# One queue for batch 0's x, a hold on GpSimd's loads, the first layer in halves, and a new order: cross-attention followed by a snake layer on one core

## The chip, the cores and the metric

The kernel runs on one NeuronCore of a Trainium2 chip. The core has TensorE (PE in the profile: matmuls and transposes into eight PSUM banks), ScalarE (ACT), VectorE (DVE), GpSimd (POOL) and SyncE (SP). Transfers are started from queues: SP and ACT start plain copies ("hardware" queues in the profile), GpSimd starts copies that also change the type from fp32 to bf16 (the "software" queue). All of them run on the same 16 DMA engines.

The metric is the time of one execution on the device in microseconds. The kernel before takes 228.31 us, the median of 3 runs (228.03 to 229.27).

## The reference

```python
x:     (8, 8, 512, 64)    # batch, head, token, dim
state: (8, 8, 32, 64)
scores = x @ state^T / sqrt(64);   a  = softmax(scores);   xread = a @ state
scores2 = state @ x^T / sqrt(64);  a2 = softmax(scores2);  sread = a2 @ x
X = concat([xread, sread], tokens) -> (8*544, 512)     # heads side by side

h = X @ w_in                    # 512 -> 2048
g = h + sin(alpha*h)**2 / (alpha + 1e-9)
out = g @ w_out                 # 2048 -> 512
```

Both softmaxes come from the same exponentials E, normalized along states for `xread` and along tokens for `sread`.

## The kernel before

**Tiling.** There are nine token tiles `t`. Tile 0 to 7 is `xread` of batch `t` (512 tokens), tile 8 holds the 256 rows of `sread` of all batches. The 2048 hidden units are 16 blocks `f` of 128. For each pair (t, f) the kernel makes `h` (two matmuls of 128x512 for a batch, four of 128x256 for tile 8), then `si` (sine on ACT), `sq` (square on ACT "A", DVE "V" or GpSimd "G"), `gt` (square times 1/alpha plus h, on DVE, which frees the PSUM bank of h). The output is made in row blocks `o.t.st`, each a chain of 16 matmuls over f into one bank, copied out by `oc` and stored by `os` on SP.

**M instead of xread.** For a batch, a @ state @ w_in is computed as A^T times M, with M = state @ w_in per pair of heads. `m.b.s` makes slice s (512 of the 2048 columns) of M in two PSUM banks, one for each half g of the contraction (four heads each), and `me` copies each to bf16. `h` then sums over g = 0 and g = 1. The A of a batch has the same two halves.

**Batch 0's start.** x of batch 0 comes in quarters (`lq`, two heads each, fp32, 256 KB), is cast and rearranged (`xq`), transposed on TensorE (`xtq`), copied to SBUF (`xc`), multiplied with the transposed state (`sc`), then `ex` (exponential on ACT), `rs` and `rr` (sum and reciprocal on DVE), `nm` (normalize on DVE or GpSimd), `at` (transpose on TensorE), `ac` (copy). State 0 comes by its own small load (`l_st0`), is transposed by `st0_t` and copied into the state tile `stT` by `st0_c`. The states of the other batches come in one load `l_st`, transposed by `st_t` and copied by `st_c`.

**The other batches.** `lx` loads x on GpSimd's queue as bf16, `pk` rearranges it on DVE, `td` transposes it by DMA on SP (batch 1 does it on TensorE, `xt`), and `ad` transposes A by DMA on SP. `w`, `cs`, `rc` and `xs` make `sread` of a batch.

**Weights.** `li.s` loads slice s of w_in (columns, 512 KB as bf16), `lo.s` loads four blocks f of w_out, all on GpSimd's queue in the order of the list.

**Order.** Each engine executes its instructions in the order in which they were emitted, and waits when an input is not there or a buffer is not free. The emission order is a written list of steps, `ORDER`, in which a step's arguments name batch, block, PSUM bank and engine. For example `h.0.7.4` is h of tile 0, block 7, in bank 4; `o.0.1.3.4` adds block 3 to row block 1 of tile 0; `m.1.3.6.3` is slice 3 of batch 1 into banks 6 and 3. There is no other scheduler. `warm_up.n.cols.bank` issues n matmuls of zeros that nothing reads. The start of the list:

```python
lq.0.A lq.1.S consts lq.2.A l_st0 zero.0 ident_ warm_up.6.512.0 zero.1 exp_table lq.3.S l_st
identf.V li.0 l_alpha xq.0.V li.1 xtq.0.1 xq.1.A li.3 xq.2.A xtq.1 xc.0.0.0.V st0_t.2 lx.1.0.1
xc.0.0.1.A xtq.2.3 st0_c.0.A warm_up.2.128.4 xq.3.V st0_c.1.A warm_up.2.128.5 lo.0 xc.0.1.0.V xtq.3
```

Lines that the profile names: L234 `lq`, L228 `l_st0`, L240 `l_st`, L248 `lx`, L255 `li`, L261 `lo`, L270 `warm_up`, L298 `st_t`, L313 `pk`, L321 `xq`, L328 `xtq`, L353 `xc`, L359 `td`, L369 `sc`, L376 `ex`, L401 `at`, L407 `ac`, L411 `ad`, L459 `m`, L467 `me`, L484 `h` of a batch, L490 `h` of tile 8, L498 `si`, L507 `sq` on ACT, L195 products on GpSimd or DVE (`sq`, `nm`), L514 `gt`, L525 `o`, L533 `oc`, L540 `os`.

Of the kernel before, what the change touches and what calls it, by code (L numbers as in the profile page):

```python
# [13 lines left out]
FP32 = mybir.dt.float32  # L14
# [19 lines left out]
sq.0.15.A xc.1.1.1.V o.0.1.0.1.7 sq.0.14.G gt.0.4 o.0.1.1.2 sc.1.1.3 si.0.12 o.0.1.2.3 gt.0.15
o.0.1.3.4 o.0.0.0.1.1 ex.1.0 sq.0.12.G o.0.0.1.2 gt.0.14 o.0.0.2.4 o.0.1.4.6 pk.1.0.V o.0.1.6.7
gt.0.12 o.0.1.7.8 h.0.13.6 ex.1.1 rs.1.0 o.0.0.4.5 o.0.2.3.4 si.0.13 o.0.2.4.5 rr.1.0 o.0.2.5.6
rs.1.1 o.0.2.6.7 nm.1.0.0.4.G m.0.2.0.4 m.1.2.2.3 rr.1.1 o.0.0.5.6 me.0.2.0.V o.0.0.6.7 nm.1.1.0.4.G
o.0.2.7.8 me.0.2.1.A me.1.2.0.V o.0.0.7.8 o.0.3.0.1.0 sq.0.13.A o.0.3.1.2 me.1.2.1.V h.0.8.4 ad.1
h.0.9.2 gt.0.13 si.0.8 h.0.10.3 si.0.9 o.0.3.2.3 sq.0.8.V o.0.3.3.4 h.0.11.6 si.0.10 gt.0.8 sq.0.9.G
o.0.3.4.6 si.0.11 o.0.3.6.7 o.0.1.8.9 sq.0.10.A h.1.2.4 gt.0.9 sq.0.11.G o.0.0.8.9 o.0.3.7.8 si.1.2  # L40
gt.0.10 h.1.12.2 lx.3.0.1 o.0.3.8.9 gt.0.11 sq.1.2.A h.1.7.3 o.0.0.9.10 si.1.12 gt.1.2 h.1.4.6
si.1.7 o.0.0.10.11 sq.1.12.V o.0.1.9.10 h.1.13.4 pk.2.0.V si.1.4 sq.1.7.G gt.1.12 o.0.1.10.11
o.0.0.11.12 si.1.13 o.0.0.12.14 sq.1.4.A o.0.0.14.15 pk.2.1.V sq.1.13.G h.1.8.2 gt.1.7 td.2
o.0.2.8.10 si.1.8 gt.1.4 o.0.0.15.16 h.1.3.3 oc.0.0.A gt.1.13 sq.1.8.G o.0.3.9.10 h.1.0.6 si.1.3
os.0.0 h.1.14.1 si.1.0 gt.1.8 sq.1.3.G o.0.1.11.13 si.1.14 h.1.1.4 h.1.5.2 sq.1.0.G si.1.1
o.0.3.10.12 si.1.5 o.0.2.10.11 sq.1.14.G o.0.1.13.15 sq.1.1.A o.0.1.15.16 o.0.3.12.14 oc.0.1.A
sq.1.5.G pk.3.1.V pk.3.0.V gt.1.3 td.3 gt.1.0 gt.1.1 h.1.6.3 h.1.9.6 os.0.1 gt.1.14 si.1.6
o.0.3.14.15 sc.2.1.7 gt.1.5 si.1.9 sc.2.0.4 sq.1.6.G o.0.2.11.13 ex.2.0 o.0.2.13.15 sq.1.9.G
o.0.2.15.16 gt.1.6 o.0.3.15.16 o.1.3.0.2.1 oc.0.2.V o.1.3.2.4 h.1.10.2 oc.0.3.A gt.1.9 os.0.2
o.1.1.0.1.3 ex.2.1 o.1.1.1.2 os.0.3 rs.2.0 h.1.11.5 si.1.10 o.1.1.2.3 rr.2.0 m.2.0.4.0.6.7 rs.2.1  # L50
nm.2.0.0.4.G o.1.1.3.4 rr.2.1 o.1.1.4.5 me.2.0.1.V o.1.1.5.6 nm.2.1.0.4.G o.1.3.4.5 me.2.1.1.A
o.1.3.5.6 o.1.1.6.7 si.1.11 o.1.3.6.7 o.1.1.7.8 sq.1.10.G me.2.1.0.V me.2.0.0.V ad.2 o.1.3.7.8
sq.1.11.A o.1.3.8.10 h.1.15.0 gt.1.11 o.1.2.0.2.7 si.1.15 o.1.2.2.3 gt.1.10 o.1.2.3.5 sq.1.15.A
o.1.2.5.6 o.1.1.8.10 gt.1.15 m.2.2.6.4.5.2 o.1.1.10.11 me.2.2.0.A me.2.2.1.V h.2.1.0 me.2.3.0.A
o.1.1.11.12 me.2.3.1.V h.2.3.6 si.2.1 o.1.1.12.14 si.2.3 h.2.13.4 sq.2.1.V h.2.0.5 gt.2.1 sq.2.3.A
w.0.2 si.2.0 gt.2.3 cs.0 h.2.2.0 si.2.13 rc.0 sq.2.0.G o.1.2.6.7 o.1.1.14.15 si.2.2 o.1.2.7.9
sq.2.13.G xs.0.0 h.2.5.6 sq.2.2.A gt.2.0 o.1.1.15.16 o.1.2.9.10 si.2.5 o.1.2.10.11 oc.1.1.V lx.4.0.1
h.2.10.5 sq.2.5.A gt.2.13 o.1.2.11.12 os.1.1 h.2.4.3 si.2.10 xs.0.1 o.1.2.12.13 o.1.0.0.1.4 gt.2.5
si.2.4 sc.3.0.2 sq.2.10.G o.1.0.1.3 gt.2.2 h.2.8.6 sq.2.4.A o.1.2.13.14 gt.2.10 h.2.15.0 si.2.8
o.1.0.3.4 gt.2.4 o.1.2.14.15 si.2.15 sq.2.8.G sc.3.1.5 o.1.0.4.5 o.1.2.15.16 ex.3.0 o.1.0.5.6  # L60
o.1.3.10.11 sq.2.15.G oc.1.2.V o.1.0.6.8 gt.2.8 o.1.0.8.9 os.1.2 o.1.0.9.10 h.2.7.3 gt.2.15
o.1.3.11.12 ex.3.1 o.1.0.10.11 pk.4.1.V o.1.3.12.13 si.2.7 o.1.0.11.12 rs.3.0 o.1.3.13.14
o.1.0.12.14 rs.3.1 m.3.2.7.6.2.0 o.1.3.14.15 pk.4.0.V o.1.3.15.16 rr.3.0 me.3.2.0.A o.1.0.14.15 td.4
rr.3.1 sq.2.7.G me.3.3.0.V h.2.11.5 oc.1.3.A o.1.0.15.16 me.3.2.1.V h.2.9.7 me.3.3.1.A nm.3.0.0.4.G
h.2.6.2 oc.1.0.A gt.2.7 o.2.0.0.1.1 os.1.3 si.2.11 o.2.0.1.2 os.1.0 nm.3.1.0.4.G o.2.0.2.3
m.3.0.0.6.4.3 si.2.9 o.2.0.3.4 si.2.6 sq.2.11.G me.3.0.1.V ad.3 o.2.0.4.6 me.3.1.1.A me.3.0.0.V
o.2.1.0.1.6 me.3.1.0.A o.2.1.1.2 sq.2.9.G o.2.1.2.3 gt.2.11 h.2.14.3 sq.2.6.A o.2.1.3.5 si.2.14
gt.2.9 sc.4.0.0 sc.4.1.4 gt.2.6 o.2.1.5.6 sq.2.14.A h.2.12.5 ex.4.0 o.2.2.0.1.7 gt.2.14 o.2.2.1.3
o.2.0.6.11 o.2.1.6.7 si.2.12 rs.4.0 o.2.0.11.12 o.2.1.7.8 h.3.0.2 rr.4.0 h.3.5.3 nm.4.0.0.4.V
# [532 lines left out]
```

The softmax here doesn't subtract the row's maximum and nothing guards it: scores larger than these inputs give would overflow.

## Time and profile before

| | |
|---|---|
| median of 3 runs | 228.31 us (228.03 to 229.27) |
| profiled execution | 228.42 us |
| its span | 226.7 us |
| busy: TensorE | 212.7 us, 94% |
| busy: ACT, DVE, GpSimd | 176.5, 162.6, 113.1 us |
| granted TensorE clock | 1.00 throughout |
| HBM read, written | 17.38 MB, 8.91 MB |
| DMA, first 26 us | 200 GB/s |
| first o matmul | 26.12 us |
| last matmul chain to end of span | 222.97 to 226.7 us |

Busy time counts the time in which at least one instruction of the engine is under way. A group's mean includes the time from issue to result, so a matmul of 512 columns is listed with some 379 ns although ten in a row take 2.16 us. In a line of the timeline the first number is the start, the second the length of the merged group, then engine, source line, operation, output and input, the count, and in brackets how long the engine had been idle and what ended that. Lines of windows give, for a stretch from A to B, the busy time and count of each engine in the order PE, PEld (weight loads), DVE, ACT, POOL, then granted clock, DMA share and GB/s. A line of a DMA queue gives packets, MB, and its share of 16 engines' time in the window; q0 is GpSimd's queue, q1 SP's and q10 ACT's.

### The profile page before, as it was taken

Reading aid. Unit: us, or ns where it says so; the run is one execution under the profiler, and the core shown is the slowest. Engines: PE = TensorE matmul, PEld = TensorE weight load, DVE = VectorE, ACT = ScalarE, POOL = GpSimd, SP = SyncE. Lnnn points to the kernel's source line nnn. Section 1 sums busy time; section 2 is a strip of 40 time slices with the busy share of each in tenths; the row PEclk is TensorE's granted clock in tenths of the full one; section 3 lists DMA queues with packets and bytes.
Section 4 is the critical chain, followed back from the end, with each engine's and each line's share of the span. In section 5 each row is a group of like instructions: output and inputs, shape, how many; then the busy total and the mean of one; then the engine's idle time right before and its main releaser. Section 6 shows DMA issues by size and latency. Waiting matters only on the chain.

```text
span 226.7 us, 4202 instructions
## 1 busy us (share of the span) xinstructions
PE 212.7 (94%) x1538; PEld 104.6 (46%) x1565; DVE 162.6 (72%) x282; ACT 176.5 (78%) x296; POOL 113.1 (50%) x123
## 2 busy tenths in 40 slices
PE   4599899999999899999999999989999999999993
PEld 1473544444444344444444444444455656557441
DVE  3268997998897958888898888798368558782000
ACT  3299988998899899889997599799573789981122
POOL 8436955885064714844965358546033329461000
PEclk9999999999999999999999999999999999999999
DMA  7999993974136730774348710870104111110222
GB/s 175 213 202 206 206 174 55 174 189 123 19 62 127 171 64 0 196 140 85 35 58 229 145 50 0 130 193 5 46 0 154 36 46 49 46 48 3 94 83 102
DMA packets 37949, 23.42 MB, mean 103 GB/s; under 512 B 21016, under 2 KB 33576, under 8 KB 37928
## 3 DMA queue, kind: packets, MB, share of 16 engines
q0 software_dynamic: 11648, 8.13, 25.1%
q1 hardware_dynamic: 25704, 14.49, 23.6%
q10 hardware_dynamic: 576, 0.53, 0.8%
q8 instruction: 12, 0.20, 0.3%
q14 instruction: 9, 0.07, 0.1%
HBM read 17.38 MB, written 8.91 MB: 116 GB/s over the span
## 4 chain that ended last, share of the span: by engine, by line
PE 65%; DVE 8%; ACT 8%; DMA 7%; POOL 6%; issue 4%; SPq 0%; POOLq 0%; ACTq 0%
PE o_ps L525 41%; PE h_ps L484 13%; POOL s L195 5%; ACT s L498 5%; DMA x<-in_x_dram 4%; DMA xnat<-in_x_dram 4%; DVE gT L514 3%; PE h_ps L490 3%; PE m_ps L459 2%; DVE xp L313 2%; PE s_ps L369 2%; PE w_ps L421 1%; ACT M L467 1%; DVE M L467 1%; PE w_ps L432 1%
## 5 line engine op out<-in xcount | busy, mean ns | idle before, releaser
L525 PE MATMUL o_ps<-w_out_sb,gT 128*128 128x512 bf16 (+1 forms) x540 | 131.6, 373 | 2.1 <-DVE gT L514 0.8
L195 POOL TENSOR_TENSOR s<-s 128x512 bf16<-128x512 bf16 (+1 forms) x88 | 86.2, 997 | 72.2 <-ACT s L498 65.6
L514 DVE SCALAR_TENSOR_TENSOR gT<-s,inva_sb,h_ps 128x512 bf16<-128x512 bf16 (+1 forms) x144 | 97.0, 713 | 21.6 <-POOL s L195 12.8
L498 ACT ACTIVATE s<-h_ps,alpha_sb 128x512 bf16<-128x512 f32 (+1 forms) x144 | 89.1, 671 | 9.9 <-PE h_ps L484 8.5
L525 PEld LDWEIGHTS <-gT 128*128 128x128 bf16 x560 | 53.0, 98 | 61.9 <-issue 4.6
L484 PE MATMUL h_ps<-AT,M 128*128 128x512 bf16 x249 | 70.3, 379 | 2.1 <-DVE M L467 0.7
L484 PEld LDWEIGHTS <-M 128*128 128x128 bf16 x256 | 24.4, 98 | 31.8 <-issue 4.7
L507 ACT ACTIVATE s<-s 128x512 bf16<-128x512 bf16 (+1 forms) x49 | 29.9, 611 | 0.8
L533 ACT COPY o_sb<-o_ps 128x512 f32<-128x512 f32 (+1 forms) x25 | 14.2, 574 | 20.1 <-PE o_ps L525 20.1
L467 ACT CAST M<-m_ps 128x512 bf16<-128x512 f32 x34 | 18.4, 594 | 5.4 <-PE m_ps L459 5.4
L195 POOL TENSOR_TENSOR A<-E,rR 128x512 bf16<-128x512 bf16 x13 | 13.4, 1047 | 17.5 <-DVE rR L386 11.8
L467 DVE CAST M<-m_ps 128x512 bf16<-128x512 f32 x30 | 19.2, 676 | 2.9 <-PE m_ps L459 2.8
L380 DVE TENSOR_REDUCE R<-E 128x16 f32<-128x512 bf16 x16 | 10.5, 664 | 3.4 <-ACT E L376 3.4
L459 PE MATMUL m_ps<-w_in_sb,stT 64*32 64x512 bf16 x256 | 10.8, 382 | 0.1
L376 ACT ACTIVATE E<-s_ps 128x512 bf16<-128x512 f32 x16 | 9.2, 599 | 1.6 <-PE s_ps L369 1.6
L498 ACT ACT_TABLE_LOAD x7 | 9.0, 1283 | 0.9 <-PE h_ps L484 0.8
L376 ACT ACT_TABLE_LOAD x7 | 9.0, 1283 | 0.1
L490 PE MATMUL h_ps<-xs_all,w_in_sb 128*128 128x256 bf16 x64 | 8.6, 272 | 0.0
L313 DVE COPY xp<-xnat 128x1024 bf16<-128x1024 bf16 x14 | 7.8, 575 | 1.1 <-DMA xnat<-in_x_dram 1.1
L533 DVE COPY o_sb<-o_ps 128x512 f32<-128x512 f32 x10 | 6.9, 686 | 2.3 <-PE o_ps L525 2.1
L439 DVE RECIPROCAL rC<-w_ps 128x128 f32<-128x128 f32 x8 | 7.5, 946 | 1.4 <-PE w_ps L432 1.4
L490 PEld LDWEIGHTS <-w_in_sb 128*128 128x128 bf16 x64 | 6.3, 98 | 2.8 <-issue 0.2
(54 smaller groups left out, 90.8 us busy)
## 6 DMA issues: line engine op xcount, KB each, us to landing
out_dram<-o_sb SPq DMA_DIRECT2D x33, 256.0 KB, 2.4
xnat<-in_x_dram POOLq DMA_DIRECT2D x7, 512.0 KB, 6.1
w_in_sb<-in_moe_w_in_dram POOLq DMA_DIRECT2D x4, 512.0 KB, 12.3
w_out_sb<-in_moe_w_out_dram POOLq DMA_DIRECT2D x4, 512.0 KB, 18.0
x<-in_x_dram ACTq DMA_DIRECT2D x2, 256.0 KB
x<-in_x_dram SPq DMA_DIRECT2D x2, 256.0 KB, 5.8
st_nat<-in_state_dram POOLq DMA_DIRECT2D x1, 256.0 KB, 7.2
out_dram<-o_sb SPq DMA_DIRECT2D x2, 128.0 KB
```

What stands on the lines that cost most here:

```text
L195: {"V": k.nc.vector, "G": k.nc.gpsimd}[eng].tensor_tensor(out, a, b, ALU.mult)
L313: k.copy(eng)(k.t["xp", b][:, :, hs, :], k.t["xnat", b][:, hs, :].rearrange("p h (i d) -> p i h d", i=k.C),)
L376: k.nc.scalar.activation(E[:, g], k.t["sc", b, g][:], ACT.Exp, scale=k.scale)
L459: k.nc.tensor.matmul(k.t["m", b, s + n, g][o0:o0 + k.Ns, :], k.stT[k.half(r), b * k.G + g, c0:c0 + k.Ns], k.w_in_sb[k.half(r), 2 * g + h, ...
L467: k.copy(eng)(k.t["M", b][:, g, s * k.FW:(s + 1) * k.FW], k.t["m", b, s, g][:])
L484: k.nc.tensor.matmul(hp[:, :n], k.t["M", t][:, g, fs], k.t["AT", t][:, g, :], start=(g == 0), stop=(g == k.G - 1),)
L490: k.nc.tensor.matmul(hp[:, :n], k.w_in_sb[:, q, fs], k.xs_all[:, q].rearrange("p b j -> p (b j)"), start=(q == 0), stop=(q == k.Q - 1),)
L498: k.nc.scalar.activation(s[:, :n], k.t["h", t, f][:, :n], ACT.Sin, scale=k.alpha_sb[:, f:f + 1])
L507: k.nc.scalar.activation(s2[:, :n], s[:, :n], ACT.Square)
L514: k.nc.vector.scalar_tensor_tensor(gT[:, :n], k.t["s2", t, f][:, :n], k.inva_sb[:, f:f + 1], k.t["h", t, f][:, :n], ALU.mult, ALU.add,)
L525: k.nc.tensor.matmul(k.t["o", t, st, half][:, cols], k.t["gT", t, f][:, rows], k.w_out_sb[:, f, cols], start=(f == 0), stop=(f == k.FT - 1),)
L533: k.copy(eng)(o_sb[:, cols], k.t["o", t, st, half][:, cols])
```

## The change

- The four quarters of batch 0's x are all issued on SP, in order, and the state of batch 0 and now also that of batch 1 are loaded by SP (`l_sf`, transposed by `sf_t`, copied by `sf_c`). `l_st` still brings all states; its copies now serve batches 2 to 7.
- A new step `hold` makes GpSimd copy one column of quarter 0, so GpSimd goes on to its loads only when that quarter has landed. The loads follow in the order w_in 0, 2, 1, x of batch 1, w_out 0, 1, all states, then (behind both `nm` of batch 0) w_in 3, w_out 2, 3, x of batch 2.
- `h` of batch 0 is issued as two steps `hg`, one for each half g of the contraction, which may stand apart in the list.
- There are 18 `warm_up` steps instead of 6: the first with 6 matmuls of 512 columns as before, then 17 with 2 of 128 columns (before 5).
- Both `nm` of batch 0 are on GpSimd (one was on DVE).
- The whole list is new. Batches are worked in the order 0, 1, 2, 3, 5, 4, 7, 6 with tile 8 (before 0 to 7, then 8 beside 7), banks and engines of the copies and squares are chosen anew (squares: 43 on ACT, 78 on GpSimd, 7 on DVE before; 48, 69, 11 after, for tiles 0 to 7; output copies of whole rows: 23 on ACT and 10 on DVE before, 15 and 18 after; M copies: 34 and 30 before, 39 and 25 after). The row block made in two halves (`oh`) is now one of tile 7.

```diff
-lq.0.A lq.1.S consts lq.2.A l_st0 zero.0 ident_ warm_up.6.512.0 zero.1 exp_table lq.3.S l_st
-identf.V li.0 l_alpha xq.0.V li.1 xtq.0.1 xq.1.A li.3 xq.2.A xtq.1 xc.0.0.0.V st0_t.2 lx.1.0.1
...
+l_alpha lq.0.S consts lq.1.S zero.0 ident_ exp_table warm_up.6.512.0 zero.1 l_sf.0.S lq.2.S identf.V
+lq.3.S l_sf.1.S xq.0.A hold li.0 xtq.0.1 xq.1.A li.2 sf_t.0.2 xc.0.0.0.V al_t.3 li.1 xq.2.A xtq.1
+sf_c.0.1.V sf_c.0.0.V al_c xtq.2.4 xc.0.0.1.A xq.3.V lx.1.0.1 inva xtq.3 xc.0.1.0.A sc.0.0.5 lo.0
+xc.0.1.1.V sf_t.1.6 ex.0.0 sc.0.1.7 lo.1 sf_c.1.1.V sf_c.1.0.A warm_up.2.128.0 rs.0.0
+warm_up.2.128.2 ex.0.1 l_st warm_up.2.128.3 warm_up.2.128.1 rr.0.0 warm_up.2.128.4 sin_table rs.0.1
+warm_up.2.128.5 nm.0.0.0.4.G m.0.0.6.0 m.1.0.2.3 rr.0.1 warm_up.2.128.7 me.0.0.1.V warm_up.2.128.1
+warm_up.2.128.4 warm_up.2.128.5 nm.0.1.0.4.G at.0.0.7 me.1.0.1.A me.0.0.0.V warm_up.2.128.1
+warm_up.2.128.4 warm_up.2.128.5 warm_up.2.128.0 ac.0.0.A warm_up.2.128.1 warm_up.2.128.4 me.1.0.0.V
+warm_up.2.128.3 li.3 at.0.1 hg.0.1.0.5 hg.0.2.0.0 ac.0.1.V m.1.2.6.1 lo.2 hg.0.3.0.4 me.1.2.0.A
+me.1.2.1.V hg.0.2.1 lo.3 hg.0.3.1 hg.0.1.1 si.0.2 m.0.2.3.2 lx.2.0.1 hg.0.0.0.7 si.0.3 me.0.2.1.V
+hg.0.0.1 me.0.2.0.A m.0.1.6.1 sq.0.3.V sq.0.2.G si.0.1 gt.0.3 hg.0.10.0.2 hg.0.9.0.3 si.0.0 hg.0.9.1
+me.0.1.0.V sq.0.1.G hg.0.10.1 hg.0.8.0.4 me.0.1.1.A hg.0.8.1 hg.0.5.0.6 si.0.10 hg.0.5.1 sq.0.0.G
+gt.0.2 gt.0.1 hg.0.4.0.1 hg.0.4.1 si.0.5 hg.0.7.0.0 hg.0.7.1 sq.0.10.A xt.1.0.5 pk.1.1.V sq.0.5.G
+gt.0.0 si.0.4 gt.0.10 xt.1.1.7 xc.1.0.1.A sq.0.4.G xc.1.0.0.V si.0.9 hg.0.6.0.2 xc.1.1.0.V hg.0.6.1
+xc.1.1.1.A gt.0.5 o.0.3.0.1.5 sq.0.9.G o.0.3.1.2 si.0.6 o.0.3.2.3 gt.0.4 o.0.3.3.4 o.0.1.0.1.7
...
-        e = k.stT[:, 0:k.G] if part == 0 else k.stT[:, k.G:]
+        e = k.stT[:, 0:2 * k.G] if part == 0 else k.stT[:, 2 * k.G:]
...
-    def l_st0(k):
-        k.st0 = k.const.tile([k.Ns, k.H, k.D], FP32, name="st0")
-        k.nc.sync.dma_start(k.st0[:], k.state[0].rearrange("h j d -> j h d"))
+    def l_sf(k, b, eng):
+        k.t["sf", b] = k.const.tile([k.Ns, k.H, k.D], FP32, name=f"sf{b}")
+        {"A": k.nc.scalar, "S": k.nc.sync}[eng].dma_start(
+            k.t["sf", b][:], k.state[b].rearrange("h j d -> j h d")
+        )
...
+    def hold(k):
+        k.nc.gpsimd.tensor_copy(k.tiny[:, 2:3], k.x0[:, 0, 0:1])
...
-    def st0_t(k, bank):
+    def sf_t(k, b, bank):
...
-    def st0_c(k, r, eng):
+    def sf_c(k, b, r, eng):
...
-        k.copy(eng)(dst[:, k.Q:, r, :, half, :], src[:, k.Q:, r])
+        k.copy(eng)(dst[:, 2 * k.Q:, r, :, half, :], src[:, 2 * k.Q:, r])
...
+    def hg(k, t, f, g, *bank):
+        if g == 0:
+            k.t["h", t, f] = k.ps(bank[0], [k.P, k.S], FP32, "h_ps")
+        k.nc.tensor.matmul(
+            k.t["h", t, f][:], k.t["M", t][:, g, f * k.P:(f + 1) * k.P], k.t["AT", t][:, g, :],
+            start=(g == 0), stop=(g == k.G - 1),
+        )
```

## The prediction

> **What bounds the kernel now.** I read the page first (engine shares, slices), then the timeline of the first 26 us, the DMA queues in half-microsecond windows, the landing times of the weights, and last the count of TensorE weight loads from the start to several times.
>
> ```profile
> PE 212.7 (94%) x1538; PEld 104.6 (46%) x1565; DVE 162.6 (72%) x282; ACT 176.5 (78%) x296; POOL 113.1 (50%) x123
> ...
> PE   4599899999999899999999999989999999999993
> ```
>
> TensorE is the bound, except in the first slices. There the timeline shows what it waits for:
>
> ```profile
> 4.08 0.62 ACT L321 CAST xp<-x 128x512 bf16<-128x512 f32 x1 [0.78 <-DMA x<-in_x_dram]
> 4.64 0.90 DVE L321 CAST xp<-x 128x512 bf16<-128x512 f32 x1 [2.33 <-DMA x<-in_x_dram]
> 5.56 0.62 ACT L321 CAST xp<-x 128x512 bf16<-128x512 f32 x1 [0.86 <-DMA x<-in_x_dram]
> 8.90 0.74 POOL L261 DMA_DIRECT2D w_out_sb<-in_moe_w_out_dram  x1 [1.37 <-DMA st_nat<-in_state_dram]
> 10.10 0.43 DVE L321 CAST xp<-x 128x512 bf16<-128x512 f32 x1 [3.00 <-DMA x<-in_x_dram]
> 12.01 1.19 ACT L376 ACTIVATE E<-s_ps 128x512 bf16<-128x512 f32 x2
> ```
>
> Three quarters of batch 0 are there by 5.6 us, the fourth at 10.1, and the first exponential follows at 12.0. The queues, in the windows 2.5:3.0 and 5.0:5.5, say why:
>
> ```profile
> q1 hardware_dynamic: 96, 0.10, 57.1%
> q10 hardware_dynamic: 78, 0.08, 44.8%
> ```
> ```profile
> q0 software_dynamic: 25, 0.05, 58.4%
> q1 hardware_dynamic: 13, 0.01, 9.6%
> ```
>
> SP's queue moves 96 packets in half a microsecond beside ACT's, and 13 once GpSimd's queue is running.
>
> ```profile
> 0.00:26.00 26.00, 19.25 (x193) 10.90 (x196) 15.24 (x34) 17.84 (x33) 16.20 (x24) 1.00 1.13 200
> ...
> 0.00:75.00 75.00, 66.87 (x519) 32.36 (x528) 59.08 (x108) 63.17 (x103) 44.70 (x52) 1.00 0.81 146
> ...
> 0.00:155.00 155.00, 145.39 (x1086) 68.50 (x1105) 127.06 (x220) 134.25 (x219) 91.11 (x98) 1.00 0.65 125
> ```
>
> The weight loads say how far the order has come. I price TensorE's steps by chain rows: an o matmul 0.216 (10 in 2.16), an h pair 0.43, a slice of M 0.28 (16 matmuls in 0.56), one sc call 0.235, w 0.47, cs 0.57, st_t 0.95, an h of the last tile 0.44. By these, the first 196 loads are worth 14.1 us at 26, 528 are worth 61.0 at 75, and 1105 are worth 139.8 at 155. The kernel is behind its own TensorE work by 11.9, 14.0 and 15.2 us. So nearly all that is lost is lost before the first o matmul at 26.12. From there 193.7 us of work remain and TensorE ends at 222.97, 196.85 later: 3.1 lost. The last copy and its store take 3.73 more, to the span of 226.7.
>
> **The change part by part.** The sum is made against the profiled execution, 228.42 (226.7 and 1.72 around it); the median of the runs, 228.31, is 0.11 below.
>
> *x on SP alone.* SP issues in 0.46 each: quarters 0 and 1 from 0.74, batch 0's state, quarters 2 and 3, batch 1's state (from 3.05). The two added issues and the second state load put 1.4 us in front of nothing else on SP, whose next work before was at 33.48. ACT loses two issues (1.04); its exponential table still ends before quarter 0 is there. 1.18 MB at the 0.13 to 0.18 MB per half microsecond that the hardware queues moved before 4.5 us, from first packets at 2.2: quarter 0 at 3.3, quarter 3 at 5.5 to 6.6. I take 6.3, as one queue alone moved 0.14 in the window 4.0:4.5.
>
> *The hold.* One GpSimd copy of a column waits for quarter 0; queued behind it are all GpSimd loads, so the first issue moves from 1.44 to about 3.5. The first load's packets came 3.1 us after its issue (1.44 to 4.5), so GpSimd's packets start at about 6.7, when quarter 3 is through. The whole st_nat load (256 KB) also goes behind five other loads. The first slice of w_in landed 9.6 us after its issue at 2.17, at 11.8; the next loads fit steps of 2.56 us (512 KB at the 205 GB/s of the windows):
>
> ```profile
> DMA to landing us min/median/max: 9.6/12.3/20.4
> ```
>
> After: w_in slice 0 at 9.8 (6.7, 2.56 and half a microsecond for completion), slice 2 at 12.4, slice 1 at 15.0, batch 1's x at 17.5, w_out's first two parts at 20.1 and 22.7, st_nat 24.0, slice 3 at 26.5, the last w_out at 31.7. Before, by the same steps: 11.8, 14.4, 16.9 for the first three slices, x 19.5, w_out 22.0, 24.6, its last 32.2. So the weights come 0.5 to 2 us earlier although they are asked for later.
>
> A rule that speaks against one queue: the Trainium skill, "DMA: Bandwidth & Descriptors", section "Queues, rings and completion order", says that every DMA engine goes round the queues packet by packet. Once GpSimd runs, two x queues would then hold two turns of three, one queue one of two. By the rule alone the sum goes towards the last rival below, 229.9; by the rows it stays, as quarter 3 is through by 6.7.
>
> *Batch 0's chain.* Quarter 3 at 6.3, cast and transposes to 7.5, scores and first exponential at 8.1 to 8.7 (12.0 before). A second state transpose sits before the second scores (0.5). Sums and reciprocals (0.69 and 0.25 each) bring the first GpSimd normalization to 9.9; the second is now also GpSimd's, 1.05 behind it instead of DVE's 0.67 beside it (to 12.0). M's first slices wait for w_in, 9.8. The second half of AT is copied at 13.2, so the first full h is at 13.4; it was 17.3 to 18.1. The split into halves lets the first half's matmul start 0.6 earlier; it adds no matmul, and I give it nothing, as ACT is the limit next. Twelve more spare matmul steps (24 matmuls, 1.3 us warm) stand before the first h, in time in which TensorE waits anyway; should they be on the path, they cost 1.3, and at the half rate of the first six (0.43 each) 2.6.
>
> A second rule: "TensorE: Matmul & The Clock Gate", Part 1, says the array runs at half rate until some 3.4 us of sustained work. In the trace four transposes take 0.61 at 14.88 and 0.40 at 15.94, which looks like that step, while the granted clock reads 1.00. By the rule, the 22 half matmuls of the first h's would cost up to 4.7 more if the array fell idle before them, and the spare matmuls prevent that; by the rows, where the longest wait is 2.75 (8.16 to 10.91), there is nothing to prevent and no term.
>
> *To the first o.* ACT then runs without a gap: M copies (0.59), sines (0.69), squares (0.64) and x copies (0.62), from 13.3: si.0.2 13.9, si.0.0 to 17.1, sq.0.10 to 19.6, the last x copies 20.8 and 22.1. DVE's gt.0.10 (0.74) after that square ends at 20.6, which frees the bank of hg.0.6; o.0.3 follows at 21.1 to 21.7, and I take 21.4 (26.12 before). Landing bounds it from below: w_out's first part, 20.1. From above: 23.4, if quarter 3 comes at 8.3.
>
> *The rest.* At the first o the new order has less behind it: 195.9 us of work remain, not 193.7 (both state transposes, 1.9, and one more slice of M, 0.28, come later). All o, h, w and cs counts are equal. Other moves: 5 M copies, 8 squares to ACT, 8 output copies from ACT to DVE, 13 squares off GpSimd, one pair of table loads fewer (2.57); ACT's sum changes by under 1 us of 176.5. ACT (78%) must now keep up with a TensorE that is 4 us nearer. I take 3.1 lost as before plus 0.4; ends 2 and 6.
>
> Sum: 21.4 + 195.9 + 3.5 = 220.8; with 3.73, span 224.5; with 1.72, 226.3; on the scale of the median **226.2**, 2.1 less than 228.31.
>
> **The rivals.**
> - *The weights bind.* If the GpSimd stream only shifts by the 2.1 of the hold, less the 1.3 that st_nat's 256 KB takes, w_in lands at 12.6 and w_out at 22.9, and the first o waits: 22.9 + 195.9 + 3.5 + 3.73 + 1.72 = 227.8. For it: the loads did share their first microseconds with x. Against: that sharing cost them throughput too, and it is gone.
> - *ACT takes it back.* ACT is busy 43.8 of the first 54 us and 63.2 of 75. If it can't give more, the lost time grows from 3.5 to 6: 228.7, no change.
> - *Late x loads (slower).* The order issues the x of batches 3 to 7 only 6.0 to 6.9 us of TensorE work before the DVE copy that reads it (before: 6.4 to 8.8). The median landing is 6.1, but the one issued at 63.99 took 8.05, and between 70 and 75 us the lag grew by 0.8. If all five land as late at 0.8 to 1.0 each, 4 to 5 us are added, of which one was in the 3.1: 229.4 to 230.3. It decides from four late loads of five. Against it: only one load of six did so.
> - *Quarter 3 is starved anyway.* If one queue can't finish x before GpSimd starts, quarter 3 comes at 10 and everything moves by 3.7: 229.9.
>
> **How the numbers follow.** Forecast 0.58 (own range 224.5 to 227.7), weights 0.12, ACT 0.11, late x 0.13, starved quarter 0.06. The range 224.2 to 230.0 runs from an early first o (20.1) with 3 lost to the slower rivals. A measurement can tell about 0.5%, 1.14 us: faster is below 227.2, slower above 229.45. Most of the forecast (0.55), a third of the weights and little of ACT are faster: 0.62. Slower: late x, starved x, a little of ACT: 0.21. The rest, 0.17.
>
> **What would show it.** Right: the last cast of x at about 6.5 without a DMA wait of 3 us; the first exponential near 8.5; first h near 13.4; first o near 21.4; a lag, in weight loads priced as above, near 8 at the first o and below 12 at the end; the same 3.7 tail. Wrong: M's first matmuls after 12 (weights), DVE copies of x waiting for DMA in batches 3 to 7, or a lag that grows by more than 5 after 25 us.

## The result and the profile after

The changed kernel takes 237.1 us (median of four runs, 235.2 to 238.2) against 228.2 for the kernel before on the same chip: a ratio of 1.038, 95% interval 1.031 to 1.046. It is 8.9 us slower; the forecast was 2.1 us faster. The profiled execution took 235.16 us, with a span of 233.2. It is the fastest of the four, so the trace shows 6.7 us of the loss; the numbers below are of that execution.

The page, with the lines that answer to those shown of before (TensorE's share, its busy tenths in 40 slices), and the chain that ended last, by engine:

```profile
PE 217.2 (93%) x1593; PEld 105.3 (45%) x1593; DVE 166.1 (71%) x289; ACT 176.8 (76%) x299; POOL 105.1 (45%) x114
...
PE   5889998999989797999999959999999999999993
...
PE 62%; DMA 17%; ACT 9%; POOL 5%; DVE 3%; issue 3%; POOLq 0%; ACTq 0%
```

The same chain of the kernel before:

```profile
PE 65%; DVE 8%; ACT 8%; DMA 7%; POOL 6%; issue 4%; SPq 0%; POOLq 0%; ACTq 0%
```

The first slices are fuller than before (5889 against 4599). But there are now dents in the middle (an 8 and two 7s in slices 12 to 16, a 5 in slice 24), where the kernel before had hardly anything under 9. And DMA holds 17% of the chain that sets the end; before it was 7%.

The timeline of the start of the changed kernel (start, length, engine, line, operation; in brackets the idle time before and what ended it):

```profile
3.78 1.38 ACT L335 CAST xp<-x 128x512 bf16<-128x512 f32 x2 [1.08 <-DMA x<-in_x_dram]
7.42 0.43 DVE L335 CAST xp<-x 128x512 bf16<-128x512 f32 x1 [0.17 <-DMA x<-in_x_dram]
9.03 0.60 ACT L390 ACTIVATE E<-s_ps 128x512 bf16<-128x512 f32 x1
...
3.93 2.42 POOL L267 DMA_DIRECT2D w_in_sb<-in_moe_w_in_dram  x3
...
12.38 1.05 PE L473 MATMUL m_ps<-w_in_sb,stT 64*32 64x512 bf16 x16 [1.06 <-DMA w_in_sb<-in_moe_w_in_dram]
13.37 1.04 PE L282 MATMUL warm_ps<-warm 128*128 128x128 bf16 x8
14.20 0.63 PE L415 MATMUL a_ps<-ident,A 128*128 128x128 bf16 x4
14.62 1.41 PE L282 MATMUL warm_ps<-warm 128*128 128x128 bf16 x14
15.87 0.39 PE L415 MATMUL a_ps<-ident,A 128*128 128x128 bf16 x4
16.10 0.59 PE L513 MATMUL h_ps<-AT,M 128*128 128x512 bf16 x2
```

x does come early: the last cast is at 7.4 instead of 10.1, the first exponential at 9.0 instead of 12.0. Then TensorE waits for the first slice of w_in (12.38), and 22 spare matmuls (1.04 and 1.41 us) stand in its queue ahead of the two transposes of A. The first half layer is at 16.1, the first o matmul at 24.8 (26.1 before): 1.3 us are won.

The windows from the start (busy time and count for PE, PEld, DVE, ACT, POOL; granted clock, DMA share, GB/s) say where it is lost again:

```profile
0.00:26.00 26.00, 21.35 (x189) 11.92 (x190) 16.34 (x36) 16.57 (x29) 17.77 (x26) 1.00 1.05 186
0.00:65.00 65.00, 58.91 (x492) 29.11 (x492) 48.93 (x92) 51.64 (x86) 37.32 (x45) 1.00 0.93 156
0.00:75.00 75.00, 68.82 (x551) 33.38 (x552) 57.21 (x105) 60.80 (x103) 44.72 (x53) 1.00 0.89 153
0.00:95.00 95.00, 86.05 (x660) 40.69 (x661) 73.29 (x131) 76.14 (x129) 52.90 (x61) 1.00 0.82 140
0.00:130.00 130.00, 121.05 (x908) 56.75 (x909) 99.35 (x175) 107.77 (x178) 70.57 (x78) 1.00 0.71 126
0.00:140.00 140.00, 128.02 (x974) 60.28 (x974) 105.96 (x187) 113.78 (x187) 72.74 (x80) 1.00 0.71 126
```

Priced as in the prediction, the weight loads are worth 15.0, 51.9, 62.0, 78.4, 113.2 and 120.1 us. The lag (the time less that work) is 11.0, 13.1, 13.0, 16.6, 16.8 and 19.9 us. From there to the end it is flat: 19.2 at 220 us. In the kernel before it went from 11.9 to 14.8 over the whole run. So the start is better, and some 8.7 us are lost between 34 and 140 us.

The waits of 34 to 145 us that DMA ended (engine, line, what was waited for; total us, times, longest), and the links of DMA in the chain that ended last (issue, us to landing):

```profile
DVE xp L327 <- DMA xnat<-in_x_dram: 4.0, 3, 2.4
...
PE s_ps L383 <- DMA xT<-xp: 3.0, 1, 3.0
...
PE h_ps L498 <- DMA AT<-A: 1.5, 2, 0.9
```
```profile
60.17 4.87 DMA AT<-A
...
80.24 10.01 DMA xnat<-in_x_dram
...
128.50 8.15 DMA xT<-xp
```

The kernel before has one such wait in that stretch, 1.1 us on DVE. Its load of x took 6.1 us to land (median), its transpose of x by DMA 4.3, that of A 3.1. Here one load of x took 10.0 and one transpose of x 8.15. Each slow one stands beside another transfer. The transpose of batch 7's x (issued at 128.50) runs while the load of batch 6's x, issued at 126.64, is under way. The load of batch 5's x (80.24) runs beside the transpose of batch 4's x, issued at 79.42. In the new order, with batches 5 and 4, 7 and 6 exchanged, loads and transposes come in pairs.

### The profile page after: what moved, and what is told of

It reads as the page before. It is cut to its first block, busy times and chain, and to the rows that moved or that the text cites. A ratio compares the mean times of both kernels' runs of the same rounds, so it can differ in the third digit from the quotient of the medians.

```text
span 233.2 us, 4272 instructions
## 1 busy us (share of the span) xinstructions
PE 217.2 (93%) x1593; PEld 105.3 (45%) x1593; DVE 166.1 (71%) x289; ACT 176.8 (76%) x299; POOL 105.1 (45%) x114
## 4 chain that ended last, share of the span: by engine, by line
PE 62%; DMA 17%; ACT 9%; POOL 5%; DVE 3%; issue 3%; POOLq 0%; ACTq 0%
PE o_ps L548 37%; PE h_ps L498 14%; DMA xnat<-in_x_dram 4%; ACT s L521 4%; DMA AT<-A 4%; DMA w_in_sb<-in_moe_w_in_dram 4%; DMA xT<-xp 3%; POOL s L201 3%; PE h_ps L504 3%; PE m_ps L473 3%; DVE R L394 1%; PE h_ps L513 1%; DMA x<-in_x_dram 1%; POOL A L201 1%; ACT L390 1%
## 5 line engine op out<-in xcount | busy, mean ns | idle before, releaser
L548 PE MATMUL o_ps<-w_out_sb,gT 128*128 128x512 bf16 (+1 forms) x560 | 137.8, 373 | 0.4 <-DVE gT L537 0.3
L201 POOL TENSOR_TENSOR s<-s 128x512 bf16<-128x512 bf16 (+1 forms) x75 | 74.8, 1009 | 75.6 <-ACT s L521 69.2
L530 ACT ACTIVATE s<-s 128x512 bf16<-128x512 bf16 (+1 forms) x57 | 34.2, 602 | 1.1
L498 PEld LDWEIGHTS <-M 128*128 128x128 bf16 x224 | 21.3, 98 | 27.8 <-DMA AT<-A 2.5
L481 ACT CAST M<-m_ps 128x512 bf16<-128x512 f32 x39 | 21.0, 592 | 10.6 <-PE m_ps L473 10.4
L201 POOL TENSOR_TENSOR A<-E,rR 128x512 bf16<-128x512 bf16 x16 | 16.5, 1048 | 25.1 <-DVE rR L400 17.2
L556 ACT COPY o_sb<-o_ps 128x512 f32<-128x512 f32 (+1 forms) x17 | 9.5, 561 | 21.2 <-PE o_ps L548 21.2
L556 DVE COPY o_sb<-o_ps 128x512 f32<-128x512 f32 x18 | 12.3, 686 | 13.1 <-PE o_ps L548 13.0
L481 DVE CAST M<-m_ps 128x512 bf16<-128x512 f32 x25 | 16.4, 678 | 5.1 <-PE m_ps L473 5.0
L383 PE MATMUL s_ps<-stT,xT 128*128 128x64 bf16 x128 | 6.6, 199 | 3.0 <-DMA xT<-xp 3.0
```

What stands on the lines that cost most here:

```text
L201: {"V": k.nc.vector, "G": k.nc.gpsimd}[eng].tensor_tensor(out, a, b, ALU.mult)
L481: k.copy(eng)(k.t["M", b][:, g, s * k.FW:(s + 1) * k.FW], k.t["m", b, s, g][:])
L498: k.nc.tensor.matmul(hp[:, :n], k.t["M", t][:, g, fs], k.t["AT", t][:, g, :], start=(g == 0), stop=(g == k.G - 1),)
L530: k.nc.scalar.activation(s2[:, :n], s[:, :n], ACT.Square)
L548: k.nc.tensor.matmul(k.t["o", t, st, half][:, cols], k.t["gT", t, f][:, rows], k.w_out_sb[:, f, cols], start=(f == 0), stop=(f == k.FT - 1),)
L556: k.copy(eng)(o_sb[:, cols], k.t["o", t, st, half][:, cols])
```

## The experiments

The theory: the start gains what the trace shows, and the time is lost because loads of x on GpSimd's queue run beside DMA transposes that TensorE or DVE is waiting for. The rivals: the spare matmuls, the halves or the new order on the engines cost it; or the hold does. All kernels compute the full reference. The kernel before took 228.4 to 228.7 us beside each group of these runs. In the diffs of the order, steps that moved stand with their neighbours.

| run | built on | us, median (range, runs) | ratio to before, 95% interval |
|---|---|---|---|
| e1: four x loads earlier | after | 229.2 (227.7 to 231.0, 10) | 1.0039 [1.0005, 1.0072] |
| e12: one x load and its copies later | after | 231.5 (229.7 to 233.8, 4) | 1.0169 [1.0131, 1.0206] |
| e10: that load earlier instead | after | 238.0 (236.6 to 239.0, 4) | 1.0396 [1.0342, 1.0450] |
| e4: no hold | after | 237.3 (236.2 to 239.4, 4) | 1.0391 [1.0332, 1.0451] |
| e8: whole first layers | e1 | 229.2 (227.8 to 230.9, 10) | 1.0027 [0.9995, 1.0059] |
| e6: no spare matmuls | e1 | 227.9 (226.6 to 228.6, 10) | 0.9965 [0.9941, 0.9990] |
| e9: a w_out slice and a transpose later | e6 | 232.8 (231.3 to 233.9, 6) | 1.0165 [1.0124, 1.0206] |
| e11: half an x load later | e6 | 230.8 (229.6 to 231.6, 6) | 1.0098 [1.0074, 1.0123] |
| e2: a load beside a transpose | before | 235.9 (234.9 to 237.0, 4) | 1.0320 [1.0277, 1.0363] |
| e3: early start | before | 230.3 (228.7 to 232.2, 8) | 1.0068 [1.0039, 1.0097] |
| e7: e3, x of batch 3 later | before | 231.7 (230.1 to 233.2, 4) | 1.0129 [1.0070, 1.0188] |
| e5: e7, a w_out slice later | before | 228.5 (227.8 to 232.2, 10) | 1.0008 [0.9980, 1.0036] |

### The x loads of the changed kernel, earlier

```diff
-oc.1.2.V lx.4.0.1 h.2.14.7
+o.1.0.2.3 lx.4.0.1 sc.3.1.1
-h.3.3.2 lx.5.0.1 si.3.2
+o.1.1.5.6 lx.5.0.1 si.2.5
-si.5.13 lx.7.0.1 h.5.5.0
+o.3.1.14.16 lx.7.0.1 me.5.1.1.A
-h.4.4.0 lx.6.0.1 si.4.2
+o.3.0.14.15 lx.6.0.1 o.3.3.8.9
```

> The changed kernel with four steps of the order moved: the x loads of batches 4, 5, 7 and 6 are issued 10 to 16 us of TensorE work earlier (at 41, 57, 97 and 104 us of that work instead of 54, 67, 104 and 113), so that they are through before the transposes by DMA that they ran beside. Theory A (late transfers: in the changed kernel's profile the lag behind TensorE's own work grows from 11 to 20 us after the first o matmul, in steps that stand at an x load or a transpose by DMA that landed late): the DVE waits for x of 1.3 and 2.4 us and the 3.0 us wait of the scores for the transpose of 8.1 us go, and the time falls by 3 to 6 us, to 230 to 233. Theory B (the vector engines can't follow an earlier start, so any lead is given back): at most 1 us less, and the lag grows by as much.

Four GpSimd loads moved, nothing else, and 7.9 of the 8.9 us are back, more than the 3 to 6 expected. The same windows of this kernel:

```profile
0.00:26.00 26.00, 20.55 (x190) 11.11 (x191) 16.96 (x37) 16.88 (x30) 17.60 (x26) 0.87 1.07 192
...
0.00:95.00 95.00, 87.75 (x681) 41.23 (x682) 75.86 (x135) 79.24 (x134) 55.93 (x64) 0.96 0.82 146
0.00:130.00 130.00, 122.75 (x937) 57.43 (x938) 102.24 (x180) 110.86 (x184) 72.57 (x80) 0.97 0.74 135
0.00:140.00 140.00, 132.75 (x1016) 62.02 (x1017) 110.94 (x197) 119.40 (x196) 76.95 (x85) 0.98 0.70 129
```

At 140 us TensorE has issued 1017 weight loads where the changed kernel had 974. The lag is 10.8, 13.7, 13.6 and 13.6 us: the start is the same, and the growth after 65 us is nearly gone. The slowest transpose of x took 5.0 us instead of 8.1. So the places of four loads made most of the loss. That doesn't tell whether they were too late or too close to another transfer.

### Late, or beside another?

Two runs move one load of the changed kernel, x of batch 6, once behind the transpose of batch 7's x (with its two copies on VectorE, which follow that transpose in both orders) and once far ahead of it.

```diff
-h.4.4.0 lx.6.0.1 si.4.2
+o.5.0.3.5 lx.6.0.1 sq.5.9.A
-o.5.0.8.9 pk.6.1.V h.4.1.6
+h.4.14.2 pk.6.1.V pk.6.0.V
```

> The changed kernel with one load moved the other way: x of batch 6 goes from 126.6 us (1.9 before the transpose of x of batch 7) to about 133, behind the landing of that transpose, with its two copies on VectorE directly ahead of its own transpose at 141. No load is made earlier, and none stands beside another. By the collision as the cause: the transpose lands in 4.3 to 5 instead of 8.15, the wait of the scores (3.0 us) goes, and the time is 234.0 (233 to 235), 3 less than the changed kernel. If lateness of loads alone is the cause: 237 to 238.

The load went out at 130.8 us instead of 126.6, later than in the changed kernel, and the time fell by 5.6 us to 231.5. The landing times of the transposes of x, and the windows to 95, 130 and 140 us:

```profile
DMA to landing us min/median/max: 4.3/4.5/5.0
```
```profile
0.00:95.00 95.00, 86.96 (x670) 40.83 (x671) 74.27 (x133) 78.39 (x132) 55.10 (x63) 0.96 0.83 146
0.00:130.00 130.00, 121.96 (x933) 57.10 (x934) 100.64 (x179) 110.01 (x182) 71.01 (x79) 0.97 0.71 131
0.00:140.00 140.00, 131.96 (x1012) 61.68 (x1013) 109.34 (x195) 118.53 (x195) 76.04 (x84) 0.98 0.70 128
```

The lag stays at 14.4 us from 95 to 140, where the changed kernel went from 16.8 to 19.9. So the load that is issued later, but alone, costs nothing, and the one beside the transpose cost 3.1 us. The other 2.4 us between the two profiles arose before 130 us, where both kernels do the same steps: the two loads of x at 67 to 90 us and the pair of transposes of A at 60 cost more in one execution than in another. The lag at 95 us was 16.6, 15.3 and 14.4 in the profiles of the changed kernel, of the next run and of this one, all with the same steps so far.

```diff
-h.4.4.0 lx.6.0.1 si.4.2
+o.3.0.14.15 lx.6.0.1 o.3.3.8.9
```

> The changed kernel with one of its four loads moved: x of batch 6 (issued at 126.6 us, 1.9 before the transpose of x of batch 7) goes 9 us of TensorE work ahead, before that of batch 7. By the collision as the cause: the transpose lands in 4.3 to 5 instead of 8.15, the 3.0 us wait of the scores goes, and the lag stays at 16.8 through 130 to 140 us: 3 us, 233.5 to 234.5. By the order of work as the cause (the same stall whatever the transfers do): 236 to 237.5.

238.0, no gain, and outside both expectations. The load went out right ahead of that of batch 7's x, both at 119.7 us, so this edit only changed what it stood beside. The transpose then took 5.0 at most, as forecast, but the chain behind x of batch 7 had to wait. The waits of 125 to 145 us:

```profile
DVE xp L327 <- DMA xnat<-in_x_dram: 5.9, 1, 5.9
PEld L498 <- DVE M L481: 5.4, 1, 5.4
```

VectorE stands 5.9 us at the copy of x, with a copy of M queued behind it that TensorE needs. The experiment didn't isolate what it was made for; it shows a second way in which the place of a load costs: one load right ahead of another that is needed first.

### One collision made in the kernel before

```diff
-o.4.1.10.11 lx.7.0.1 gt.5.3
+sc.5.0.7 lx.7.0.1 pk.6.0.V
```

> The kernel before with one step moved: the x load of batch 7 is issued just ahead of the transpose by DMA of batch 6's x instead of 23 us of TensorE work later. No work is added. Theory A: that transpose lands after some 8 us instead of 4.3, the scores of batch 6, which follow 4.6 us of TensorE work later, wait about 3 us, and the time rises by 2 to 3 us, to 230 to 231. If such a collision is covered elsewhere: 228.3, no change. Theory B says no change too.

7.5 us slower, more than twice the forecast. The transpose of batch 6's x, in the chain that ended last, and the waits of 100 to 140 us:

```profile
118.63 9.52 DMA xT<-xp
```
```profile
PE s_ps L369 <- DMA xT<-xp: 4.6, 1, 4.6
```

In the kernel before the same transposes took 4.3 to 5.0 us. The load of x had been issued 0.4 us ahead of it. TensorE waited 4.6 us for it; the lag went from 14.4 at 120 us to 20.9 at 135, and stayed. So one load in one wrong place is enough for most of what the change lost.

The rule on arbitration that the prediction weighed for x (the Trainium skill, "DMA: Bandwidth & Descriptors", "Queues, rings and completion order": each DMA engine takes turns between its queues by packets) bears on this case too. With two busy queues a transfer would get every other turn; an estimate by the rule is twice the undisturbed 4.3 us, 8.6. The runs show 8.15 and 9.52. The two queues of this run from 122 to 123 us, and then SP's in the kernel before from 120 to 121, where the same transpose runs alone:

```profile
q0 software_dynamic: 238, 0.12, 87.8%
q1 hardware_dynamic: 239, 0.06, 46.3%
```
```profile
q1 hardware_dynamic: 834, 0.21, 110.9%
```

The queues did take turns packet by packet, 238 to 239. But the transpose went at 239 packets per microsecond instead of 834, less than half, until the load was through at 125 us, and its first packets went after 121 us instead of after 119. So the estimate comes near the landing times, though the trace adds up to them differently. How much the stores on SP's queue added in the changed kernel is not separated.

### Where the early start goes

The hold was taken out of the changed kernel.

```diff
-xq.0.A hold li.0
+xq.0.A li.0
```

> The changed kernel without the hold, so that GpSimd's loads are issued from about 1.4 us on. Theory A: w_in's first slice lands at 10 to 11 instead of 12.35, the fourth quarter of x one to three us later than 7.3, first o within 1 us of 24.8, and the time stays at 234 to 238, as the loss is later. If the hold is the loss: 232 or less.

Without it the last cast of x is at 12.2 us instead of 7.4, the first exponential at 13.8 instead of 9.0, the first o at 28.5 instead of 24.8 (expected within 1 us of it). The medians are the same, 237.3 against 237.1; the two profiled spans, 235.5 and 233.2, keep 2.3 of the 3.7 us. So the hold is worth 0 to 2 us here, less than the lead that it gives. In the other direction, the early start was given to the kernel before:

```diff
-lq.0.A lq.1.S consts lq.2.A l_st0
-exp_table lq.3.S l_st
+lq.0.S lq.1.S l_st0 lq.2.S lq.3.S consts
+exp_table hold l_st
```

> The kernel before with two parts of the change alone: the four quarters of batch 0's x on SP in order (with batch 0's state after the second), and the hold ahead of GpSimd's loads, whose order stays (all states, w_in 0, 1, 3). Theory A: the last cast of x is at about 7.4 instead of 10.1, the first exponential at about 9.5 instead of 12.0, but w_in's first slice comes at about 13.5 and the first h no earlier than 16.5, so the time is within 1.5 us of before, 227 to 229.5. If these two parts are themselves what makes the changed kernel slow: 232 or more.

The first o comes at 23.2 us, 3.0 earlier, with the first h at 14.3 where 16.5 at the earliest was expected, and the time is 1.6 us longer by the ratio, 1.8 by the medians, just above the expected range. The lead is lost at one place: the lag goes from 9.8 at 34 us to 15.7 at 42. (The profiled execution took 232.1 us, 1.8 above the median; that of the next run shows the same stall.) The chain that ended last and TensorE's wait at the layer of batch 1:

```profile
30.51 7.50 DMA AT<-A
```
```profile
PE h_ps L487 <- DMA AT<-A: 4.4, 1, 4.4
```

The transposes of batch 1's A are issued 3.0 us earlier than before (33.48) and land later: 38.0 instead of 36.6. The last of GpSimd's first stream of loads (weights, state, x of batches 1 and 2) arrives only at about 37 us; the hold had started it 2.4 us later. At 34.6 us the load of batch 3's x joins it. Two runs separate the two.

```diff
-h.1.12.2 lx.3.0.1 o.0.3.8.9
+o.0.2.10.11 lx.3.0.1 sq.1.14.G
-pk.3.1.V pk.3.0.V td.3 gt.1.0
+ad.2 pk.3.1.V pk.3.0.V td.3
```

> As the run with the shorter first stream, but all of w_out stays in that stream: only x of batch 3 (issued at 34.6 us, within the transposes of A of batch 1, with the early start) goes behind the transpose of x of batch 2. If the end of the first stream holds the transposes: they land at 37 to 38 again, and the time is 229 to 230. If the load of x of batch 3 holds them: they land at 34 to 35, the wait for them falls under 2 us, and the time is 226 to 227.

With x of batch 3, its copies and its transpose out of the way the transposes of A take just as long (issued at 30.66, 7.58 us), TensorE waits 4.5, and the time is 231.7. So it isn't that load. Next, the last slice of w_out went behind as well:

```diff
-st_c.0.0.V lo.3 st_c.0.1.A
+o.0.0.8.9 lo.3 o.0.3.7.8
```

> The kernel before with the early start (x on SyncE's queue in order, GpSimd's loads held, first o at about 23.2 us), and with the last w_out slice and x of batch 3 issued behind the transposes of A of batch 1, and the transpose of x of batch 3 behind that of A of batch 2. Theory (the first GpSimd stream ends when it ends, and a transpose issued inside it waits for its end): the stream loses 512 KB of its end, 2.5 us at the 205 GB/s that it moved, and ends at about 34.5 us instead of 37; the transposes of A of batch 1, issued at 30.5, land at 34 to 35 instead of 38.0; the wait for them falls from 4.4 us to 1 to 2; 4 us are won on the early start alone: 226.3, 2 below the kernel before. Rival (the early start is taken back by the engines whatever the transfers do): the transposes land earlier, and the time stays at 229 to 230.

```profile
31.43 4.16 DMA AT<-A
```
```profile
PE o_ps L528 <- DMA w_out_sb<-in_moe_w_out_dram: 1.8, 1, 1.8
...
PE h_ps L487 <- DMA AT<-A: 1.0, 1, 1.0
```

The transposes land in 4.2 us and the wait falls from 4.5 to 1.0. So the end of the first stream is what held them. But the slice that was moved is now late itself (1.8), and 228.5 is no better than before. Of the 2 us forecast nothing came: the lag rises by 1.1 at the transposes, by 1.9 at the slice, and by 1.2 at the load of batch 4's x, which is late in the kernel before too (8.05 us there).

### The spare matmuls and the halves

```diff
-warm_up.2.128.0 ... warm_up.2.128.3
+(all 17 steps of 128 columns left out)
```

> The changed kernel with its four x loads earlier, without the 17 pairs of spare matmuls (128 columns). Counted work on TensorE falls by 1.3 us; in the changed kernel they took 2.4 us in the stretch from 13.3 to 16.1, ahead of the transposes of A. If they only delay: first o 1 to 2 us earlier, and the time 227.5 to 228.5, unless the transposes of A of batch 1 (issued 32.8, landed at 37.4, at the end of the first stream) take it back, which leaves 229. If they keep the clock up: granted clock under 0.9 between 8 and 20 us and no gain, or a loss of up to 1.

Without them the kernel is at 227.9 us, some 1.2 below e1 (which ran on another chip) and the only version under the kernel before. The 0.35% is less than the 0.5% that I said can be told from no change, though its interval doesn't reach 1. The timeline of TensorE at the first layer, without spares and then, in the changed kernel, with them:

```profile
13.38 0.59 PE L412 MATMUL a_ps<-ident,A 128*128 128x128 bf16 x4 [0.67 <-ACT AT L418]
14.19 0.63 PE L510 MATMUL h_ps<-AT,M 128*128 128x512 bf16 x1 [0.22 <-PE a_ps L412]
14.75 0.63 PE L470 MATMUL m_ps<-w_in_sb,stT 64*32 64x512 bf16 x8
15.31 1.76 PE L510 MATMUL h_ps<-AT,M 128*128 128x512 bf16 x4
```
```profile
16.62 0.41 PE L473 MATMUL m_ps<-w_in_sb,stT 64*32 64x512 bf16 x8
16.96 1.04 PE L513 MATMUL h_ps<-AT,M 128*128 128x512 bf16 x4
```

Four half matmuls take 1.76 us without the spares and 1.04 with them, a slice of M 0.63 and 0.41. This fits the rule of the prediction's second place (half rate until some 3.4 us of sustained work): without them the half rate lasts until 17.07, 3.7 us after the gap of 0.67 that ends at 13.38. So in these two executions the spares save five matmuls and a slice of M at half rate, about 1.2 us. They don't do it every time: in e10, with all of them, that slice still took 0.63 at 17.78, 5.1 us after TensorE's last gap had ended (12.63).

In exchange they take 2.45 us of TensorE's queue, but that delayed little. What the first layer waits for is the first slice of w_in, here in e1 and in e6:

```profile
12.04 1.05 PE L472 MATMUL m_ps<-w_in_sb,stT 64*32 64x512 bf16 x16 [1.16 <-DMA w_in_sb<-in_moe_w_in_dram]
```
```profile
11.03 1.05 PE L470 MATMUL m_ps<-w_in_sb,stT 64*32 64x512 bf16 x16 [1.07 <-DMA w_in_sb<-in_moe_w_in_dram]
```

The first layer of e6 comes 1.4 us earlier than that of e1 (14.2 and 15.6), but 1.0 of it is that slice; e8, with spares and on e6's chip, had it at 11.14. From there to the first o it is 12.4 us in e1 and in e6 (to 24.45 and 23.46) and in the changed kernel (12.38 to 24.79). So at the first o the profiles show no cost of the spares, and that the 1.2 us of the medians are theirs isn't shown.

```diff
-hg.0.2.0.0 ... hg.0.2.1
+h.0.2.0
```

> The changed kernel with its four x loads earlier, and the first layer of batch 0 in whole products (both contraction halves in one step at the place of the second half). If the halves matter: a first half can start when the first half of A has its transposes, ahead of the second; without them the first product moves from 16.1 to about 16.9, and the time rises by 0.5 to 1. If not: the same within 0.5, 229 again.

All 16 blocks of batch 0 are changed so. The first o comes 2.1 us later (26.5 against 24.5), although the first slice of w_in was there 0.9 us earlier, and the span of the profiled execution is 1.7 longer, but the median is the same: 229.2 and 229.2. In the medians the halves are worth nothing; the two profiles leave up to 1.7, but that of e8 is of an execution 1.0 above its median and that of e1 of one 0.7 below.

### Two tries to better the best

Both take bytes out of the first stream of e6, where the transposes of batch 1's A took 6.5 us (31.76 to 38.2) and TensorE waited 2.8 at its weight loads.

```diff
-hg.0.2.1 lo.3 hg.0.3.1
+sq.0.12.G lo.3 o.0.1.8.9
-o.0.0.12.13 td.2 h.1.1.0
+h.1.8.1 td.2 sq.1.6.A
```

> The run without spare matmuls (x loads earlier), with the last w_out slice issued behind the transposes of A of batch 1 (about 36 us; its first use is at about 39) and the transpose of x of batch 2 some 2.6 us later, clear of the load of x of batch 3. If the end of the first GpSimd stream is what holds those transposes (issued 31.8, landed 38.3, TensorE waited 2.8): they land at 35 to 35.5, the wait falls under 0.5, the late slice costs 0.5 to 1, and the time is 226.0 (225 to 227), 1% below the kernel before. If something else holds the lag at its level, the slice or the engines that make M and A take the place of the wait: 227.5 to 228.5.

```profile
37.40 5.43 DMA w_out_sb<-in_moe_w_out_dram
```
```profile
PE o_ps L545 <- DMA w_out_sb<-in_moe_w_out_dram: 3.3, 1, 3.3
```

The transposes of A landed in 4.8 at most, as forecast, and the lag at 38 us was 11.5 instead of 14.1. But GpSimd issued the slice at 37.4, not 36, and it landed at 42.8, after its first use was due; the load of batch 3's x went out right behind it (38.2), the next transpose of x at 40.4, and the slowest one took 8.3. The lag was 17.9 at 50 us; 232.8.

```diff
-m.0.2.3.2 lx.2.0.1 hg.0.0.0.7
+m.0.2.3.2 lx.2.0.2 hg.0.0.0.7
+sq.0.12.G lx.2.1.2 o.0.1.8.9
```

> The run without spare matmuls (x loads earlier), with the second half of x of batch 2 taken out of the first GpSimd stream and issued at about 37 us. If the bytes of the first stream set when the transposes of A of batch 1 land (38.3 with all of them): 256 KB less at 205 GB/s is 1.25 us, they land at 37.0, the wait of TensorE falls from 2.8 to about 1.5, and the time is 226.7 (226 to 227.5), provided that the late half lands before its copy at 41.5. If the wait goes over to that copy or to x of batch 3 behind it: 228 to 229.

230.8. The transposes of A no longer hold TensorE, but the late half and the load of batch 3's x went out together at 38.2, DVE waited 4.0 us for x, and a transpose of x took 7.1. In both the wait only moved to the next transfer.

## Why the prediction was wrong

The profiled span, by the prediction's own terms: first o 24.8, remaining work 195.9, lost time 8.5 (the last matmul chain ends at 229.18), tail 4.0: 233.2. Forecast were 21.4, 195.9, 3.5 and 3.73: 224.5. So 5.0 of the 8.7 us of error in the span lie in "the rest" and 3.4 in the first o.

- *"The rest", 3.1 lost as before plus 0.4.* This is the step that failed. It took over the lost time of another order as if it belonged to the engines, and looked for its growth at ACT. In its place the runs showed lost time of 8.5 us, which grew by transfers: TensorE waits 4.5 us for DMA transposes after 34 us, and its waits for DVE come to 2.7, 2.4 of them behind a DVE that had just waited for x (75.8 and 90.3 us); with four x loads moved (e1) 7.9 of the 8.9 us are back. The prediction counted the transpose and load steps by their distance to their readers and never laid loads and DMA transposes side by side in the new order.
- *The late x loads, the rival that ended on the slower side.* Right in sign, and its sign in the profile (DVE's copies waiting for DMA) was there: 4.0 us. It was under-sized: 0.8 to 1.0 for each late load against 3.1 for one transposed x here and 6.5 of lag in e2. And its mechanism was half right. It held that loads were issued too close to their own copies; e12 issued one still later and won.
- *First o at 21.4.* Quarter 3 came at 7.4 instead of 6.3, the first exponential at 9.0 instead of 8.1 to 8.7: nearly right. The first w_in slice was given 6.3 us from issue to landing (3.5 to 9.8), by full speed from the first packet; it took 8.4 (3.93 to 12.3), as the queue moved some 0.14 MB per microsecond from 7 to 11 us and 0.20 after that. So it landed 2.5 us later than forecast, most of the 3.4 us by which the first o was late. That is the "weights bind" rival's 12.6.
- *The spare matmuls, no term.* At the first o this held: they stood 2.45 us in the queue, near the 2.6 given for cold matmuls on the path, but the first o came 12.4 us after the first slice of w_in with them and without them. That there was nothing to prevent did not hold: without them 1.2 us of half rate are to be seen.
- *The halves, nothing.* Right in the medians.
- *The start carries through.* The sum added the won time at the first o to the end unchanged. In e3 a first o that is 3.0 earlier gave 1.6 to 1.8 us more: batch 1 can't begin before the transposes of its A, and these land when GpSimd's first stream is through. In e4 and e8 a first o that is 3.7 and 2.1 later left the medians within 0.2 us, and the profiles 2.3 and 1.7 longer; so at best part of a lead arrives.
- *ACT takes it back; quarter 3 is starved.* Neither was seen. ACT's busy time is 176.8 us (176.5 before).

What stays open: 2.4 us of the difference between the changed kernel and e12 arose in steps that the two share, and why a given pair of transfers costs more in one execution than in another isn't explained. Nor is it explained how the end of the first stream holds the transposes of A with so few bytes: in e7 GpSimd's queue moved 0.02, 0.01 and 0.00 MB from 35 to 38 us, and SP's 0.07, 0.07 and 0.04, where it moved 0.21 from 35 to 36 in the kernel before. It was not tried whether transposes on another engine would avoid it. The 1.9 us by which the median lies above the profiled execution was not traced.

## What to carry to other kernels

Before a new order is judged by its engines, lay its transfers on one time axis: every load that shares the DMA engines with a transpose, with both ends, and who reads each. Here a transpose that takes 4.3 us alone and is issued just in time cost 3.1 us in one kernel and 6.5 in another when a 512 KB load ran beside it, and a load moved out of the way paid only where it didn't meet the next one. An earlier start brought little here as long as the next stage's own transfer didn't land earlier too; ask what that one waits for before counting the gain.

## What the runs showed that I had not expected

- A load issued later made the kernel 5.6 us faster (e12), and one moved into the wrong place made another kernel 7.5 us slower (e2).
- Transposes issued 3.0 us earlier landed 1.4 us later (30.51 to 38.0 against 33.48 to 36.6).
- The granted clock read 0.57 from 8 to 16 us in the run e12, with all spare matmuls, and 1.00 in e6 without any:

```profile
8.00:16.00 8.00, 6.49 (x79) 4.95 (x74) 4.34 (x9) 4.47 (x8) 5.57 (x7) 0.57 1.23 190
```
```profile
8.00:16.00 8.00, 6.03 (x59) 3.18 (x59) 5.63 (x13) 5.03 (x9) 5.67 (x8) 1.00 1.25 196
```

Yet the matmuls ran at half rate in both: four transposes of A took 0.63 at 14.05 in e12, where the row reads 0.50 from 10 to 14 us, and 0.61 at 12.10 in e6; at full rate they take 0.39 (15.51 in e12). So in this stretch a row of 1.00 didn't mean full rate.
